# A causal convolution by Toeplitz matmuls moved from 64x128 to 64x64 tiles of TensorE, in front of an RWKV channel mix

## The chip, the core and the metric

The kernel runs on one core of a Trainium2 chip. The metric is the device time of one execution in microseconds (us), over several runs. The profile is one execution taken by the hardware profiler. Its engines are PE (TensorE, matmuls; PEld its weight loads), ACT (ScalarE), DVE (VectorE), POOL (GpSimd) and SP (SyncE, which here only issues DMA).

## The reference

Eight sequences of 4160 tokens with 192 channels. First a causal depthwise convolution with 7 taps: the 192 channels are 8 heads of 24, and all channels of a head share their taps, which come from a softmax over the head's 7 weights.

```python
w = softmax(weight)                       # (8 heads, 7 taps)
x_pad = concat(zeros(6 tokens), x)        # causal
y[b, s, h, g] = sum_k w[h, k] * x_pad[b, s + k, h, g]
```

Then the channel mix of RWKV on y:

```python
y_prev = y shifted by one token
xk = mu_k * y + (1 - mu_k) * y_prev       # mu: one value per channel
xr = mu_r * y + (1 - mu_r) * y_prev
k = max(xk @ w_k, 0)                      # 192 -> 1024
v = (k * k) @ w_v                         # 1024 -> 192
out = sigmoid(xr @ w_r) * v               # w_r: 192 -> 192
```

## The kernel before

The sequences go in four pairs; the two of a pair (index `s`, or `st`) lie on partitions 0 to 63 and 64 to 127 when their channels are contracted 64 at a time. TensorE therefore works in tiles of 64 rows x 128 columns: two of them, one on either half of the partitions, run side by side in the array.

**Steps, slots, bundles.** A pair is cut into steps of 512 tokens (256 at the two ends of the first pair). A step has 8 slots, each computing 128 of the 1024 channels of k for both sequences. Four slots make a bundle, so that a step takes two bundles. There are 65 bundles, then the rest of V. The program writes every engine's instructions in the order of the text below (the schedule is manual).

**PSUM.** All results of matmuls go through one ring of four tiles. A tile is two banks wide, [...]. The fifth tile takes the place of the first, and so on.

```python
ring = ctx.enter_context(tc.tile_pool(name="ring", bufs=4, space=bass.MemoryType.PSUM))
... ring.tile([P, 2, BANK], FP32, tag="k", ...)        # P = 128, BANK = 512
```

**The convolution.** x is loaded in groups of up to 10 blocks. A block has 128 tokens on the partitions, of which 120 are new (`BLK = 120`, 6 are the halo). `toe[:, h, :]` is the banded Toeplitz matrix of head h, 128 x 128. The contraction over the 128 tokens of a block is done in two halves of 64 rows (`i`), both of which add to the same outputs. Two row tiles that run side by side write different banks: in the first half of a unit, row tile i writes bank i, in the second half they change places. Between the halves a nop on ACT (`clobber_nop`) makes the second wait for the first, so that no two row tiles meet in one bank. A group of 10 blocks has four units of two heads; `conv_out` casts the unit's results to bf16 and puts the channels in the order that the mix needs.

```python
groups = []                       # (pair, first block, blocks, first bundle that needs it, on_pe)
for p in range(NPAIR):
    blk0 = 0
    for nb, s, on_pe in (
        ((3, 0, True), (4, 1, True), (4, 2, True), (5, 3, True), (10, 4, False), (9, 6, False))
        if p == 0
        else ((10, 0, False), (10, 2, False), (10, 4, False), (5, 7, False))
    ):
        groups.append((p, blk0, nb, first_bundle[first_step[p] + s], on_pe))
        blk0 += nb

def conv_units(g):                # heads that go into bank 0 and bank 1
    if groups[g][2] * 4 * G <= BANK:                      # up to 5 blocks
        return [((0, 1), (6, 7)), ((2, 3), (4, 5))]
    return [((0,), (1,)), ((3,), (4,)), ((6,), (7,)), ((2,), (5,))]

def conv_mm(g, c, half):
    ...
    for k in range(last + 1):
        for i in range(2):
            q = slice(i * Q, (i + 1) * Q)                 # Q = 64
            bank = (i + half) % 2
            h = unit[bank][k]
            nc.tensor.matmul(                             # line 300
                out=banks[:, bank, :, :, k * G : (k + 1) * G],
                lhsT=toe[q, h, :],
                rhs=xbs[g][q, :nb, :, h * G : (h + 1) * G],     # nb * 2 * 24 columns
                start=half == 0 and k == 0, stop=half == 1 and k == last)
    if half == 0:
        nc.scalar.clobber_nop([nc.scalar.lower_ap(conv_ps[g, c])])
```

The groups marked `on_pe` (the first four of the first pair) get to the mix by TensorE alone. The others ("large groups") go by way of DRAM: y is written there token by token (`y_write`) and read back transposed (`y_read`), channels on the partitions.

**K, R and V.** A k tile is three pairs of 512-column matmuls, followed by a relu on ACT and a square on DVE. R of 256 tokens is six pairs of 192 columns, followed by a sigmoid on ACT. V is 32 pairs of 192 columns in two halves, with the same change of banks and the same nop between them, and is multiplied by R's sigmoid on DVE.

```python
def k_relu(n):
    ...
    nc.scalar.activation(out=k_sb, in_=ps..., func=AF.Relu)          # line 499
def r(s, j):
    ps = ring.tile(...)
    ...                                                             # matmuls: line 544
    r_sbs[s, j] = three.tile([P, 2, 2 * D], BF16, tag="r_sb", name="r_sb")
    nc.scalar.activation(out=r_sbs[s, j], in_=ps[:, :, 0 : 2 * D], func=AF.Sigmoid)
def v_rows(s, j, half, ks=(0, 1)):
    ...                                                             # matmuls: line 572
    if half == 0:
        nc.scalar.clobber_nop([nc.scalar.lower_ap(v_ps[s, j])])
```

**A bundle** (`units` are the units of the convolution that this bundle has; `run(mix_...)` are DVE's steps of the mix; the parts for bundle 2 are cut):

```python
def bundle_rest(b, ns):
    units = xt.get(b, []) + [None, None]
    quad = vq.get(b, [None])[0]
    for n in bundles[b - 1][2:]:
        k_square(n)
    run(mix_a, b)
    k_mm(ns[0]); k_relu(ns[0]); k_square(ns[0])
    run(mix_b, b)
    conv_half(units[0], 0)          # first half of a unit
    k_mm(ns[1])
    conv_half(units[0], 1)          # second half, then its casts on ACT
    k_relu(ns[1]); k_square(ns[1])
    run(rq, b)                      # R; from bundle 7 on, of the next bundle's V
    v_rows(*quad, 0)
    k_mm(ns[2]); k_relu(ns[2])
    conv_half(units[1], 0)
    v_rows(*quad, 1)
    conv_half(units[1], 1)
    run(mix_c, b)
    k_mm(ns[3]); k_relu(ns[3])
    v_out(*quad)                    # the product with R on DVE, and the store
    run(late, b)
```

In the first pair the units of the large groups stand in bundles 2 to 5, two in each. In the other pairs a group's units stand one in each of successive bundles, from ten bundles before the group is needed: `xs = range(fb - 10, fb - 10 + nx)`. In bundles 6 to 53 this makes 42 bundles with one unit and 6 with none; bundles 54 to 64 have none.

Of the kernel before, what the change touches and what calls it, by code (L numbers as in the profile page):

```python
# [14 lines left out]
def kernel(  # L15
# [11 lines left out]
    nc = tc.nc  # L27
# [9 lines left out]
    HALO = K - 1  # L37
    BLK = 120
    GB = 10
    NBLK = -(-S // BLK)  # L40
    BANK = 512
    STEP = 512
    TAIL = S % 128
# [42 lines left out]

    groups = []
    for p in range(NPAIR):
        blk0 = 0
        for nb, s, on_pe in (  # L90
            ((3, 0, True), (4, 1, True), (4, 2, True), (5, 3, True), (10, 4, False), (9, 6, False))
            if p == 0
            else ((10, 0, False), (10, 2, False), (10, 4, False), (5, 7, False))
        ):
            groups.append((p, blk0, nb, first_bundle[first_step[p] + s], on_pe))
            blk0 += nb


    xbs = {}

    def x_tile(g):
        p, blk0, nb, _, _ = groups[g]
        xb = three.tile([P, GB, 2, D], BF16, tag="xb", name="xb")
        xbs[g] = xb
        if g > 4:

            nc.vector.memset(xb[0:1, 0, 0, 0:2], 0.0)
        if blk0 == 0:
            nc.gpsimd.memset(xb[0:32, 0, :, :], 0.0)
        if blk0 + nb == NBLK:  # L110
            nc.gpsimd.memset(xb[:, nb - 1, :, :], 0.0)

    def load_x(g):
        p, blk0, nb, _, _ = groups[g]
        xb = xbs[g]
        for s in range(2):
            b = 2 * p + s
            lo, hi = 0, nb
            if blk0 == 0:
                lo = 1  # L120
                nc.gpsimd.dma_start(out=xb[HALO:P, 0, s, :], in_=x[b, 0 : P - HALO, :])
            t0 = blk0 * BLK - HALO
            if blk0 + nb == NBLK:
                hi = nb - 1
                r0 = t0 + hi * BLK
                nc.gpsimd.dma_start(out=xb[0 : S - r0, hi, s, :], in_=x[b, r0:S, :])
            nc.gpsimd.dma_start(  # L127
                out=xb[:, lo:hi, s, :],
                in_=bass.AP(
                    tensor=x.tensor,  # L130
                    offset=x.offset + (b * S + t0 + lo * BLK) * D,
                    ap=[[D, P], [BLK * D, hi - lo], [1, D]],
                ),
            )

    def load_x_first(eng, q0, q1, n0, n1, s0, s1):

# [138 lines left out]
    ys, yTs, y_drams = {}, {}, {}  # L276
    conv_ps = {}

    def conv_units(g):

        if groups[g][2] * 4 * G <= BANK:
            return [((0, 1), (6, 7)), ((2, 3), (4, 5))]
        return [((0,), (1,)), ((3,), (4,)), ((6,), (7,)), ((2,), (5,))]
# [42 lines left out]
                        )  # L326

    def to_yT(g, c, o, b0, b1, copy):
        c0 = YC + (groups[g][1] + b0) * BLK
        copy(out=yTs[0][:, c, c0 : c0 + (b1 - b0) * BLK], in_=o[:, 0 : (b1 - b0) * BLK])  # L330

    def conv_out(g, c, copy):
# [24 lines left out]
            )  # L357

    def new_yT(p):
        yTs[p] = two.tile([P, 3, -(-(YC + NBLK * BLK) // 16) * 16], BF16, tag="yT", name="yT")  # L360
        y_drams[p] = dram.tile([NBLK * BLK, 2 * D], BF16, tag=f"y{p % 2}", name="y_dram")
        nc.vector.memset(yTs[p][:, :, 0:YC], 0.0)


    def y_write(g):
        p, blk0, nb, _, _ = groups[g]
        if blk0 == 0:
            new_yT(p)
        nc.sync.dma_start(
            out=y_drams[p][blk0 * BLK : (blk0 + nb) * BLK, :].rearrange("(n t) c -> t n c", t=BLK),  # L370
            in_=ys[g][:BLK, :nb, :],
        )

    def y_read(g):
        p, blk0, nb, _, _ = groups[g]
        r0, r1 = blk0 * BLK, min((blk0 + nb) * BLK, S)
        nc.sync.dma_start_transpose(
            out=yTs[p][:, :, YC + r0 : YC + r1], in_=y_drams[p][r0:r1, :]
        )


    def tr(g, j):

        p, blk0, nb, _, _ = groups[g]
        ps = ring.tile([P, 2, 2 * BANK], BF16, tag="k", name="ps_t")
        todo = range(4 * j, min(nb, 4 * j + 4))
        view = ps[:, :, 0 : 6 * BLK].rearrange("p b (c i t) -> p b c i t", c=3, i=2)
        for i0 in todo[::2]:
            for c in range(3):
                for i in range(i0, min(nb, i0 + 2)):  # L390
                    nc.tensor.transpose(
                        out=view[:, (i - 4 * j) // 2, c, i % 2, :],
                        in_=ys[g][:BLK, i, c * P : (c + 1) * P],
                        identity=ident[:BLK, :BLK],
                    )

        for i in todo[::2]:
            n = min(2, nb - i)
            c0 = YC + (blk0 + i) * BLK
            (nc.scalar.copy if g == 3 and j == 0 else nc.vector.tensor_copy)(  # L400
                out=yTs[p][:, :, c0 : c0 + n * BLK].rearrange("p c (n t) -> p c n t", n=n),
                in_=view[:, (i - 4 * j) // 2, :, :n, :],
            )
# [116 lines left out]
            vb = max(vb, last_bundle[s]) + 1  # L520
            quads.append((s, j, vb))

    r_sbs = {}

    def v_mm(o, s, t):
        for f in range(NF):
# [9 lines left out]
    def r(s, j):  # L536
        xr = xrs[s]
        ps = ring.tile([P, 2, BANK], FP32, tag="k", name="ps_r")
        for k in range(2):
            ts = slice((2 * j + k) * P, (2 * j + k + 1) * P)  # L540
            for c in range(NC):
                for i in range(2):
                    q = slice(i * Q, (i + 1) * Q)
                    nc.tensor.matmul(  # L544
                        out=ps[:, i, k * D : (k + 1) * D],
                        lhsT=xr[q, c, ts],
                        rhs=wr[q, c, :],
                        start=c == 0,
                        stop=c == NC - 1,
                    )  # L550
        r_sbs[s, j] = three.tile([P, 2, 2 * D], BF16, tag="r_sb", name="r_sb")
        nc.scalar.activation(out=r_sbs[s, j], in_=ps[:, :, 0 : 2 * D], func=AF.Sigmoid)  # L552

    v_ps = {}

# [65 lines left out]
            )  # L621


    early, rq, xt, mix_a, mix_b, mix_c, vq, late = ({} for _ in range(8))

    def at(table, b, fn, *a):
        table.setdefault(b, []).append((fn, a))
# [4 lines left out]
            if half == 1:  # L632
                conv_out(*unit, nc.scalar.copy)

    for g, (p, blk0, nb, fb, on_pe) in enumerate(groups):
        if g < 3:
            continue
        nx = len(conv_units(g))
        if p == 0:
            xs = {3: [1, 1], 4: [2, 2, 3, 3], 5: [4, 4, 5, 5]}[g]  # L640
        else:
            xs = range(fb - 10, fb - 10 + nx)
        for i, b in enumerate(xs):
            xt.setdefault(b, []).append((g, i))
        if not on_pe:
            at(late, xs[-1], y_write, g)

            at(mix_c if g == 4 else late, xs[-1] + (1 if g < 6 else 2), y_read, g)
        if g > 4:

            b = {5: 1, 6: 2, 7: 7}.get(g)
            b = first_bundle[first_step[p]] + (-15, -11, -7, -3)[(g - 6) % 4] if b is None else b
            table = {5: mix_a, 7: mix_c}.get(g, early)
            at(table, b, x_tile, g)
            at(table, b, load_x, g)
# [28 lines left out]
            at(late, fb - 1, keep_tail, p)  # L684
    for s, j, vb in quads:
        at(rq, vb if vb < 7 else vb - 1, r, s, j)
        if s == LAST:
            at(late, vb, v_last, s, j)
        else:
            vq.setdefault(vb, []).append((s, j))  # L690
# [117 lines left out]

    def bundle_rest(b, ns):

        units = xt.get(b, []) + [None, None]
        quad = vq.get(b, [None])[0]
        for n in bundles[b - 1][2:]:
            k_square(n)
# [3 lines left out]
        k_square(ns[0])  # L818
        if b > 2:
            run(mix_b, b)  # L820
            conv_half(units[0], 0)
        k_mm(ns[1])
        if b > 2:
            conv_half(units[0], 1)
        k_relu(ns[1])
        if b > 2:
            k_square(ns[1])
        run(rq, b)
        if quad:
            v_rows(*quad, 0)  # L830
        if b == 2:
            tr(3, 0)
            tr(3, 1)
            k_square(ns[1])
            run(mix_b, b)
        k_mm(ns[2])
        k_relu(ns[2])
        if b == 2:
            v_rows(*quad, 1, (0,))
            k_mm(ns[3])  # L840
            k_relu(ns[3])
            conv_half(units[0], 0)
            v_rows(*quad, 1, (1,))
            run(mix_c, b)
            v_out(*quad)
            conv_half(units[0], 1)
            conv_half(units[1], 0)
            conv_half(units[1], 1)
        else:
            conv_half(units[1], 0)  # L850
            if quad:
                v_rows(*quad, 1)
                conv_half(units[1], 1)
            run(mix_c, b)
            k_mm(ns[3])
            if not quad:
                conv_half(units[1], 1)
            k_relu(ns[3])
        if quad and b > 2:
            v_out(*quad)  # L860
# [2 lines left out]
    with tc.manual_schedule():  # L863
        prologue()
        for b in range(-20, 0):
            for table in (early, rq, xt, mix_a, mix_b, mix_c, vq, late):
                assert b not in table, b
        for b in range(quads[-1][2] + 1):
            run(early, b)
# [6 lines left out]
            else:  # L876
                if b == len(bundles):
                    for n in bundles[-1][2:]:
                        k_square(n)
                run(rq, b)  # L880
                for q in vq.get(b, ()):
                    v(*q)
                    v_out(*q)
# [31 lines left out]
```

## Time and profile before

| | |
|---|---|
| time, median of 3 | 417.19 us (417.04 to 417.88) |
| span of the profiled execution | 416.1 us |
| granted TensorE clock | 0.998 |
| mean DMA rate | 155 GB/s |

A page of the profile lists the share of the span in which each engine is busy, then groups of instructions: line, engine, operation, output <- inputs, partitions x elements, count | busy us, mean ns of one | idle time of the engine just before them, and what ended most of it. A timeline lists instructions in order of time: start in us from the span's start, length, engine, line, operation, and how many in a row are put together; a bracket at the end gives idle time ahead of it and who ended it. Matmuls are pipelined: the next one starts before the last one has ended, so that the time of a stretch is read from the starts.

### The profile page before, as it was taken

How to read it: one execution, taken by the hardware profiler on the slowest of the kernel's cores; microseconds unless marked ns; L12 is line 12 of the kernel's file. 1: busy time of each engine (PE TensorE's matmuls, PEld its weight loads, DVE VectorE, ACT ScalarE, POOL GpSimd, SP SyncE). 2: the span in 40 equal slices, each digit the busy share in tenths (PEclk: the TensorE clock that was granted, in tenths of full speed). 3: DMA queues.
4: the chain of work that ended last, by engine and by line, in shares of the span. 5: the costliest groups of instructions: out<-in, count | busy, mean ns of one | idle time of the engine just before them, and what ended most of it. 6: DMA issues, size and time to landing. Idle time of an engine off the chain costs nothing.

```text
span 416.1 us, 16339 instructions
## 1 busy us (share of the span) xinstructions
PE 407.4 (98%) x7125; PEld 317.2 (76%) x7126; DVE 377.8 (91%) x671; ACT 348.2 (84%) x409; POOL 50.7 (12%) x77
## 2 busy tenths in 40 slices
PE   7999999999999999999999999999999999999995
PEld 5567777777878777777777877777787778777795
DVE  5979799999999999999999999999999999999973
ACT  6899888889888888988988898898898788877771
POOL 8640003002030100202021010202000000000000
PEclk9999999999999999999999999999999999999999
DMA  9999889968499793959689593898856464421123
GB/s 143 174 191 204 163 221 189 237 146 163 124 185 215 170 196 102 180 155 176 167 166 206 149 218 106 140 212 166 170 101 161 131 147 125 119 79 55 61 80 115
DMA packets 134298, 64.59 MB, mean 155 GB/s; under 512 B 84158, under 2 KB 134226, under 8 KB 134226
## 3 DMA queue, kind: packets, MB, share of 16 engines
q1 hardware_dynamic: 95138, 48.32, 45.3%
q0 software_dynamic: 38288, 14.66, 31.1%
q8 instruction: 56, 0.92, 0.9%
q10 hardware_dynamic: 800, 0.57, 0.5%
q14 instruction: 16, 0.13, 0.1%
HBM read 29.89 MB, written 36.99 MB: 161 GB/s over the span
## 4 chain that ended last, share of the span: by engine, by line
PE 92%; DVE 3%; ACT 2%; DMA 1%; issue 1%; SPq 0%; ACTq 0%
PE ps_v L572 40%; PE ps_k L487 38%; PE ps_r L544 7%; PE ps_c L300 5%; ACT k_sb L499 1%; PE ps_v L527 1%; DMA mu_raw<-in_moe_mu_r_dram 1%; DVE d L425 1%; DVE k L513 1%; ACT y L346 1%; DVE o_sb L588 0%; DVE xr L461 0%; DVE xk L438 0%; DVE yT L330 0%; PE ps_t L320 0%
## 5 line engine op out<-in xcount | busy, mean ns | idle before, releaser
L499 ACT ACTIVATE k_sb<-ps_k 128x1024 bf16<-128x1024 f32 x260 | 261.3, 1040 | 53.3 <-PE ps_k L487 52.5
L487 PE MATMUL ps_k<-xk,wk 64*128 64x512 bf16 (+1 forms) x1632 | 200.7, 368 | 0.5 <-ACT k_sb L499 0.3
L513 DVE TENSOR_TENSOR k<-k_sb 128x1024 bf16<-128x1024 bf16 x260 | 177.9, 688 | 15.0 <-ACT k_sb L499 7.8
L572 PE MATMUL ps_v<-wv,k 64*128 64x192 bf16 x4032 | 189.0, 243 | 0.3 <-ACT y L346 0.2
L572 PEld LDWEIGHTS <-k 64*128 64x128 bf16 x4032 | 172.6, 94 | 13.4 <-issue 0.8
L487 PEld LDWEIGHTS <-wk 64*128 64x128 bf16 x1632 | 88.4, 94 | 50.7 <-issue 0.4
L588 DVE TENSOR_TENSOR o_sb<-ps_v,r_sb 128x768 f32<-128x768 f32 x64 | 61.2, 957 | 11.6 <-PE ps_v L572 5.3
L552 ACT ACTIVATE r_sb<-ps_r 128x768 bf16<-128x768 f32 x65 | 54.8, 846 | 0.0
L127 POOL DMA_DIRECT2D xb<-in_x_dram x34 | 30.6, 903 | 192.7 <-PE ps_c L300 93.1
L346 ACT CAST y<-ps_c 120x960 bf16<-120x960 f32 (+4 forms) x67 | 50.7, 788 | 1.8 <-PE ps_c L300 1.8
L544 PEld LDWEIGHTS <-xr 64*128 64x128 bf16 x780 | 36.0, 94 | 11.1 <-DVE xr L467 0.3
L544 PE MATMUL ps_r<-wr,xr 64*128 64x192 bf16 x780 | 43.9, 243 | 0.0
L300 PE MATMUL ps_c<-xb,toe 64*128 64x480 bf16 (+2 forms) x240 | 39.2, 335 | 0.8 <-DMA xb<-in_x_dram 0.4
L461 DVE TENSOR_SCALAR xr<-d,mu 128x512 bf16<-128x512 bf16 (+1 forms) x102 | 35.6, 354 | 0.0
L425 DVE TENSOR_TENSOR d<-yT 128x1536 bf16<-128x1536 bf16 (+3 forms) x37 | 31.4, 849 | 1.5 <-ACT yT L330 1.3
L461 DVE TENSOR_SCALAR xk<-d,mu 128x512 bf16<-128x512 bf16 (+1 forms) x98 | 32.7, 361 | 0.1
L467 DVE TENSOR_TENSOR xr<-xr,yT 128x1536 bf16<-128x1536 bf16 (+1 forms) x33 | 31.0, 939 | 1.1
L467 DVE TENSOR_TENSOR xk<-xk,yT 128x1536 bf16<-128x1536 bf16 (+2 forms) x34 | 30.4, 897 | 0.1
L300 PEld LDWEIGHTS <-toe 64*128 64x128 bf16 x240 | 13.5, 94 | 13.0 <-issue 1.6
L409 POOL COPY y_tail<-yT 128x195 bf16<-128x195 bf16 x4 | 1.7, 425 | 68.8 <-DMA yT<-y_dram 68.8
L320 PEld LDWEIGHTS <-xb 128*32 128x32 bf16 (+3 forms) x264 | 5.4, 120 | 2.1 <-ACT xb L221 1.1
L320 PE MATMUL ps_t<-toe,xb 128*32 128x120 bf16 (+3 forms) x264 | 6.6, 273 | 0.2 <-DVE toe L270 0.2
(56 smaller groups left out, 57.6 us busy)
## 6 DMA issues: line engine op xcount, KB each, us to landing
out_dram<-o_sb SPq DMA_DIRECT2D x128, 192.0 KB, 2.6
y_dram<-y SPq DMA_DIRECT2D x10, 900.0 KB, 7.0
xb<-in_x_dram POOLq DMA_DIRECT2D x14, 480.0 KB, 7.9
xb<-in_x_dram POOLq DMA_DIRECT2D x6, 432.0 KB, 8.5
xb<-in_x_dram POOLq DMA_DIRECT2D x10, 192.0 KB, 4.9
y_dram<-y SPq DMA_DIRECT2D x3, 450.0 KB
y_dram<-y SPq DMA_DIRECT2D x1, 810.0 KB
xb<-in_x_dram POOLq DMA_DIRECT2D x2, 384.0 KB, 10.4
```

The lines of the kernel that those rows point to most:

```text
L300: nc.tensor.matmul(out=banks[:, bank, :, :, k * G : (k + 1) * G], lhsT=toe[q, h, :], rhs=xbs[g][q, :nb, :, h * G : (h + 1) * G], start=hal ...
L346: copy(out=bass.AP(tensor=y.tensor, offset=y.offset + d0, ap=[y.ap[0], [d1 - d0, 2], [2 * D, nb], [Q, 2], [1, n]],), in_=bass.AP(tensor=ps ...
L425: nc.vector.tensor_tensor(out=shaped(s, diffs[s][:, cs, :L]), in0=y_of(s, cs, 1), in1=y_of(s, cs, 0), op=ALU.subtract)
L461: nc.vector.tensor_scalar(out=t[:, c, :L], in0=diffs[s][:, c, :L], scalar1=mu[:, i, c : c + 1], scalar2=None, op0=ALU.mult)
L467: nc.vector.tensor_tensor(out=o, in0=o, in1=y_of(s, sl, 0), op=ALU.add)
L487: nc.tensor.matmul(out=ps[:, i, f * L : (f + 1) * L], lhsT=wk[r, c, fs], rhs=xk[r, c, :L], start=c == 0 and f == 0, stop=c == NC - 1 and f ...
L499: nc.scalar.activation(out=k_sb, in_=ps.rearrange("p a b -> p (a b)"), func=AF.Relu)
L513: nc.vector.tensor_tensor(out=o, in0=i, in1=i, op=ALU.mult)
L544: nc.tensor.matmul(out=ps[:, i, k * D : (k + 1) * D], lhsT=xr[q, c, ts], rhs=wr[q, c, :], start=c == 0, stop=c == NC - 1,)
L552: nc.scalar.activation(out=r_sbs[s, j], in_=ps[:, :, 0 : 2 * D], func=AF.Sigmoid)
L572: nc.tensor.matmul(out=v_ps[s, j][:, bank, k * D : (k + 1) * D], lhsT=k2s[s][q, f, t * P : (t + 1) * P], rhs=wv[q, f, :], start=half == 0 ...
L588: nc.vector.tensor_tensor(out=o_sb.rearrange("p (b t) d -> p b (t d)", b=2), in0=v_ps.pop((s, j)), in1=r_sbs.pop((s, j)), op=ALU.mult,)
```

## The change

Each large group's convolution goes into tiles of 64 rows x 64 columns, [...]. The tokens are cut into sub-blocks of 56 new tokens with 64 rows each (`HB = 56`), so that a contraction of 64 rows gives a whole result: nothing is added across the halves, and the nop goes. A group of nb blocks now has 2 nb sub-blocks, half of them on the upper 64 partitions. For one head four matmuls cover the group: by the half of the partitions (`i`, which is also the bank) and by the half of the blocks (`j`, which is the half of the output's partitions). Each has nb / 2 * 48 columns. A large group of 10 holds 1120 tokens instead of 1200, and the last groups become larger to make up for it: 10 instead of 9 blocks in the first pair, 8 instead of 5 in the others. All have four units of two heads.

As a change between tilings is not free, two units stand together in one stretch behind k1, and, from the second pair on, only in every second bundle. The second unit's casts and R's sigmoid come behind the nop between the halves of V, so that the nop is not held up by them. Loads of x come in two parts for the two halves of the partitions, and writes of y in four.

```diff
-            ((3, 0, True), (4, 1, True), (4, 2, True), (5, 3, True), (10, 4, False), (9, 6, False))
+            ((3, 0, True), (4, 1, True), (4, 2, True), (5, 3, True), (10, 4, False), (10, 6, False))
             if p == 0
-            else ((10, 0, False), (10, 2, False), (10, 4, False), (5, 7, False))
+            else ((10, 0, False), (10, 2, False), (10, 4, False), (8, 6, False))
 ... (load_x)
+        if on_pe:
+            parts, step, rows = ((0, base),), BLK, P
+        else:
+            parts, step, rows = ((0, base), (Q, base + nb * HB)), HB, Q
 ... (new)
+    def conv_tiles(g, c):
+        nb = groups[g][2]
+        ...
+        ps = ring.tile([P, 2, BANK], FP32, tag="k", name="ps_c")
+        m = nb // 2
+        banks = ps[:, :, 0 : m * 4 * G].rearrange("p i (m s c) -> p i m s c", m=m, s=2)
+        for k in range(2):
+            h = 2 * c + k
+            for i in range(2):
+                q = slice(i * Q, (i + 1) * Q)
+                for j in range(2):
+                    nc.tensor.matmul(
+                        out=banks[j * Q : (j + 1) * Q, i, :, :, k * G : (k + 1) * G],
+                        lhsT=toe[q, h, q],
+                        rhs=xbs[g][q, j * m : (j + 1) * m, :, h * G : (h + 1) * G],
+                        start=True,
+                        stop=True,
+                    )
+    def conv_tiles_out(g, c):
+        ...   # one cast for units 0 and 3, two for units 1 and 2
 ... (y_write)
-        nc.sync.dma_start(
-            out=y_drams[p][blk0 * BLK : (blk0 + nb) * BLK, :].rearrange("(n t) c -> t n c", t=BLK),
-            in_=ys[g][:BLK, :nb, :],
-        )
+        for j in range(2):
+            for i in range(2):
+                r0 = base + (i * nb + j * m) * HB
+                nc.sync.dma_start(
+                    out=y_drams[p][r0 : r0 + m * HB, :].rearrange("(n t) c -> t n c", t=HB),
+                    in_=ys[g][j * Q : j * Q + HB, i * m : (i + 1) * m, :],
+                )
 ... (r: the sigmoid goes into a function of its own)
+    def r_out(s, j):
 ... (schedule)
-            xs = range(fb - 10, fb - 10 + nx)
+            xs = [fb - 9] * 2 + [fb - 7] * 2
 ... (bundle_rest, without the parts for bundle 2)
         k_square(ns[0])
         if b > 2:
             run(mix_b, b)
-            conv_half(units[0], 0)
         k_mm(ns[1])
-        if b > 2:
-            conv_half(units[0], 1)
         k_relu(ns[1])
         if b > 2:
             k_square(ns[1])
+            for u in units:
+                conv_tiles(*u)
+            for u in units[:1]:
+                conv_tiles_out(*u)
         run(rq, b)
         if quad:
             v_rows(*quad, 0)
+        if b > 2:
+            for u in units[1:]:
+                conv_tiles_out(*u)
+        run(rs, b)                  # R's sigmoid
         k_mm(ns[2])
         k_relu(ns[2])
-            conv_half(units[1], 0)
             if quad:
                 v_rows(*quad, 1)
-                conv_half(units[1], 1)
             run(mix_c, b)
             k_mm(ns[3])
             k_relu(ns[3])
```

## The prediction

> **What bounds the kernel now.** I read the page's busy shares first, then the timeline of TensorE (PE) in the middle and near the end, then ScalarE (ACT) in the same windows, and last the starts of single matmuls in the trace.
>
> ```profile
> PE 407.4 (98%) x7125; PEld 317.2 (76%) x7126; DVE 377.8 (91%) x671; ACT 348.2 (84%) x409; POOL 50.7 (12%) x77
> L300 PE MATMUL ps_c<-xb,toe 64*128 64x480 bf16 (+2 forms) x240 | 39.2, 335 | 0.8 <-DMA xb<-in_x_dram 0.4
> L346 ACT CAST y<-ps_c 120x960 bf16<-120x960 f32 (+4 forms) x67 | 50.7, 788 | 1.8 <-PE ps_c L300 1.8
> ```
>
> PE is the bound. Its 39.2 us in the convolution (L300) is not what the convolution costs, because overlapping matmuls are counted by their pipelined ends. Starts tell the cost: between the starts of successive pairs of 64-row tiles lie 215.7 ns for 512 columns (k) and 82 ns for 192 (R and V). [...] so 480 columns are 202.5 ns. From 76 us to 406 us the starts follow this sum without one gap over 30 ns: **PE streams, and only columns cost**. A whole bundle from the middle, PE (start, length, engine, line, operation):
>
> ```profile
> 202.43 1.48 PE L487 MATMUL ps_k<-xk,wk 64*128 64x512 bf16 x12
> 203.73 0.38 PE L300 MATMUL ps_c<-xb,toe 64*128 64x480 bf16 x2
> 203.93 0.83 PE L487 MATMUL ps_k<-xk,wk 64*128 64x512 bf16 x6
> 204.58 0.38 PE L300 MATMUL ps_c<-xb,toe 64*128 64x480 bf16 x2
> 204.78 0.68 PE L544 MATMUL ps_r<-wr,xr 64*128 64x192 bf16 x12
> 205.29 1.50 PE L572 MATMUL ps_v<-wv,k 64*128 64x192 bf16 x32
> ```
>
> The first twelve are k3 of the bundle before and k0, six each (3 x 215.7 = 0.65 us), so this bundle starts at T = 203.08: k0, half a unit, k1, the other half, R at T+1.70, V at T+2.21. The next one starts at 209.22: 6.14 us. ACT meanwhile:
>
> ```profile
> 203.30 1.94 ACT L499 ACTIVATE k_sb<-ps_k 128x1024 bf16<-128x1024 f32 x2 [0.80 <-PE ps_k L487]
> 205.12 0.97 ACT L346 CAST y<-ps_c 120x960 bf16<-120x960 f32 x1
> 205.96 1.06 ACT L499 ACTIVATE k_sb<-ps_k 128x1024 bf16<-128x1024 f32 x1
> ```
>
> Relu 3 of the bundle before starts at T+0.22 (its matmuls have just ended), relu 0 at T+1.14, the cast at T+2.04, relu 1 at T+2.88. ACT instructions in a row start 0.91 us apart (relu), 0.84 (cast of 960), 0.69 (sigmoid). So **ACT is at its busiest just after T**: three k tiles reach it in 1.9 us of PE time and cost it 2.7. V is close behind: relu 0 ends at 205.24, and V starts at 205.29 in the buffer that relu 0 has freed.
>
> Near the end no convolution is left:
>
> ```profile
> 347.68 2.12 PE L487 MATMUL ps_k<-xk,wk 64*128 64x512 bf16 x18
> 349.62 0.68 PE L544 MATMUL ps_r<-wr,xr 64*128 64x192 bf16 x12
> 350.12 1.50 PE L572 MATMUL ps_v<-wv,k 64*128 64x192 bf16 x32
> ...
> 353.40 2.12 PE L487 MATMUL ps_k<-xk,wk 64*128 64x512 bf16 x18
> ```
>
> Here k3, k0 and k1 run on; from one such run to the next it is 5.73 us, with the same relus and VectorE work. So neither ACT nor VectorE holds a bundle without convolution above 5.73.
>
> Two early stretches show what the change will meet. First, a switch of tiling:
>
> ```profile
> 16.99 0.83 PE L487 MATMUL ps_k<-xk,wk 64*128 64x256 bf16 x12 [0.31 <-ACT k_sb L499]
> 17.75 0.60 PE L320 MATMUL ps_t<-toe,xb 128*32 128x120 bf16 x32
> 18.29 0.39 PE L487 MATMUL ps_k<-xk,wk 64*128 64x256 bf16 x4
> ```
>
> The last k pair starts at 17.536, so the next start was due at 17.645 and came at 17.755: 0.110 us to go in. The last set of four starts at 18.135, 18.188 was due, 18.291 came: 0.103 us to go out. Inside, sets of four 120-column matmuls are 52.5 ns apart: four column tiles stream at once, and their short weight loads hide.
>
> Second, bundle 6, where two R tiles follow k1, so that V takes the fifth buffer after the convolution:
>
> ```profile
> 50.99 1.38 PE L544 MATMUL ps_r<-wr,xr 64*128 64x192 bf16 x24
> 52.55 1.17 PE L572 MATMUL ps_v<-wv,k 64*128 64x192 bf16 x24 [0.18 <-ACT y L346]
> ```
>
> ```profile
> 49.68 1.96 ACT L499 ACTIVATE k_sb<-ps_k 128x1024 bf16<-128x1024 f32 x2
> 51.50 0.99 ACT L346 CAST y<-ps_c 120x960 bf16<-120x960 f32 x1
> ```
>
> Tiles here are k0, c, k1, R, R', V. Relu 0 ends at 51.64; R' starts at 51.69. The cast ends at 52.49; V starts at 52.545. **Each tile waits for the reader of the fourth tile before it, and begins 0.05 us after that reader ends.** These waits cost PE 0.21 and 0.36 us.
>
> [...] in the trace the four of the set at 17.755 start within 10 ns. [...]
>
> **The change, part by part.**
>
> Removed from PE: in the large groups 80 pairs of 480 columns (16.2 us), 8 of 432 (1.46) and 24 of 240 (2.46), 20.1 us. Added: each head of a unit is one set of four 64x64 matmuls. Pair 0 has 2 groups x 8 heads = 16 sets of 240 columns; each other pair 3 x 8 = 24 of 240 and 8 of 192. That is 88 x 102.5 ns + 24 x 82.5 ns = 11.0 us. **Columns save 9.1 us.** There are 28 stretches (4 in pair 0, 8 in each other pair); each goes in and out: 28 x 0.213 = 6.0 us. Were nothing else moved, PE would gain **3.1 us**.
>
> Moved: the order in the ring. A bundle with convolution now takes k0, k1, c, c', R, V, k2, k3. The fourth tile before R is k0 of the same bundle, and the fourth before V is k1. Before, they were k3 of the last bundle and k0. From T on, with the measured steps:
> - PE alone: k0 and k1 end at 1.30, +0.11 switch, +0.41 for four sets, +0.10 switch: R would start at 1.92, V at 2.41.
> - ACT: relu 3 at 0.22, relu 0 at 1.14, relu 1 at 2.04 (where the cast stood). With 1.02 to 1.03 us each they end at 1.24, 2.16 and 3.07.
> - R waits for relu 0: 2.21. V waits for relu 1: **T+3.12**, 0.71 us after PE could have begun.
> - Then first half of V 1.32, k2 0.65, second half 1.32, k3 0.65: next bundle at T+7.06.
>
> Nothing else in it waits longer. The first cast follows relu 1 at 2.95 and ends by 4.0, k2 needs its buffer at 4.44. The nop that separates V's halves falls at about 4.65, V's second half is due at 5.09; this is what the sigmoid behind the nop is for, and it costs nothing, since the R of this bundle is used in the next. Second cast 4.65, sigmoid 5.5, relu 2 6.2, relu 3 at 7.28: ACT has caught up. A bundle without convolution keeps 5.73.
>
> In bundles 6 to 53: after, 24 x 7.06 + 24 x 5.73 = 306.8 us. Before, 42 bundles carried a unit and 6 none: 42 x 6.14 + 6 x 5.73 = 292.2, and 0.57 of waits in bundle 6, which go. **That is +14.0 us.** In pair 0 (bundles 2 to 5) the wait between halves in bundle 2 goes and its columns shrink (-0.5), while bundles 3 to 5 take 1.33 us for convolution and wait in place of 0.73 to 0.96 (with 0.3 us of old waits), and in bundle 3 ACT still has bundle 2's casts before relu 0 (about 0.5 more): +1.5, some **+1.0** together. Sum: 417.2 + 14.0 + 1.0 = **432 us**.
>
> Off the path: ACT gets 14 x 6 = 84 casts in the large groups for 64, some 8 us more; loads come in twice as many pieces and read 128 rows for 112 new tokens, where it was 128 for 120; writes of y come in four pieces. All have whole bundles of time: from pair 1 on a load is issued four to six bundles ahead, and y is read two bundles after it is written.
>
> **The rivals.**
> 1. The columns decide and the ring does not bite: 417.2 - 3.1, about 414, or 413.5 with bundle 6's waits gone. For it: PE has been at its columns for 330 us, and the change was arranged in stretches to save switches. Against it: V starts today within 0.05 us of its buffer's release, and bundle 6 shows the very wait. It would need ACT to reach relu 1 by T+1.3, when k1's matmuls have only just been issued.
> 2. The ring bites and ACT does not catch up: 1.75 us of casts in one bundle push relu 2 and relu 3 beyond the next T. My sum leaves ACT free at 7.1 against relu 3 ready at 7.28, so 0.2 us of slack. If 0.3 us is missing in each of 24 bundles: 439.
> 3. Transfers: more and smaller pieces make the early groups late (the load of the first large group was already waited for at 27.4 us). Worth 1 us once; later loads have slack.
> 4. Sets of 64x64 that do not overlap fully (205 ns for a set instead of 102.5): the wait for relu 1 would hide the 0.41 us more per stretch, so the total hardly moves.
>
> **Range and chances.** The wait of 0.71 us is a difference of measured steps; 0.1 us in it is 2.4 us of the total. That gives 429 to 435; rival 2 stretches the top, and a part of rival 1 (ACT ahead of my walk in some bundles) the bottom: 423 to 437. Slower by over 2% means above 425.5: 0.80. Within 2%: 0.18, nearly all rival 1. Faster than 408.8 needs more than the columns can give: 0.02.
>
> **What would show each step.** In the middle, bundles alternate 7.06 and 5.73 us. The sets of 64x64 matmuls start 102.5 ns apart, with 0.11 and 0.10 us around the stretch (the last hidden in R's wait). R's first matmul starts 0.05 us after the end of relu 0, V's after that of relu 1, 3.1 us after k0's; PE shows idle time released by ACT k_sb ahead of R and V in these bundles. ACT's casts of ps_c rise from 67 to 87 (84, and 3 of the one group that keeps the old way). Alternation at 6.35 and 5.73 would show the ring step wrong; a first V start much later than relu 1's end would point to rival 2 or to something that I don't see.

## The result, and the profile after

The changed kernel takes **432.26 us** (median of 4, 432.0 to 432.38) against 417.53 us for the kernel before, measured beside it: a ratio of 1.0351, with a 95% interval of 1.0333 to 1.0369. It is 3.5% slower. The profiled execution spans 430.5 us.

The lines of the page after that answer to those shown of before: busy shares, then the matmuls of R, V and the convolution, and the casts. (L302 and L319 are the new 64x64 convolution and its casts, L601 is R, L632 is V, L556 the relu.) The second line is the chain that ended last, by engine.

```profile
PE 409.9 (95%) x7349; PEld 313.4 (73%) x7350; DVE 373.0 (87%) x671; ACT 355.4 (83%) x429; POOL 65.1 (15%) x102
...
PE 74%; ACT 12%; issue 5%; DMA 4%; POOL 2%; SPq 1%; DVE 1%; ACTq 0%; DVEq 0%; POOLq 0%
...
L632 PE MATMUL ps_v<-wv,k 64*128 64x192 bf16 x4032 | 189.1, 243 | 6.7 <-ACT k_sb L556 6.6
...
L319 ACT CAST y<-ps_c 128x960 bf16<-128x960 f32 (+5 forms) x84 | 54.0, 684 | 21.7 <-PE ps_v L632 21.7
...
L601 PE MATMUL ps_r<-wr,xr 64*128 64x192 bf16 x780 | 43.6, 243 | 6.1 <-ACT k_sb L556 6.1
...
L302 PE MATMUL ps_c<-xb,toe 64*64 64x240 bf16 (+1 forms) x448 | 16.6, 265 | 0.0
```

The convolution itself has become cheap: 16.6 us busy for the large groups, where L300 had 39.2 (some 1.5 of these for the small group that stays). But R and V now have idle time ahead of them, and what ends it is ACT's relu. ACT is 12% of the chain that ended last. Before, it was 2%:

```profile
PE 92%; DVE 3%; ACT 2%; DMA 1%; issue 1%; SPq 0%; ACTq 0%
```

The idle figures, 6.1 and 6.7 us, are too small: a matmul's modelled end covers a part of the wait (243 ns is listed for one of V, and its pairs start 82 ns apart). Starts show all of it, 10.7 and 11.5 us. A bundle without units and one with two, PE:

```profile
203.61 2.12 PE L544 MATMUL ps_k<-xk,wk 64*128 64x512 bf16 x18
205.56 0.68 PE L601 MATMUL ps_r<-wr,xr 64*128 64x192 bf16 x12
...
209.34 2.12 PE L544 MATMUL ps_k<-xk,wk 64*128 64x512 bf16 x18
211.39 0.60 PE L302 MATMUL ps_c<-xb,toe 64*64 64x240 bf16 x16
212.19 0.67 PE L601 MATMUL ps_r<-wr,xr 64*128 64x192 bf16 x12 [0.20 <-ACT k_sb L556]
213.11 1.50 PE L632 MATMUL ps_v<-wv,k 64*128 64x192 bf16 x32 [0.24 <-ACT k_sb L556]
...
216.39 1.91 PE L544 MATMUL ps_k<-xk,wk 64*128 64x512 bf16 x16
```

And ACT in the bundle with two units:

```profile
210.20 2.85 ACT L556 ACTIVATE k_sb<-ps_k 128x1024 bf16<-128x1024 f32 x3 [0.82 <-PE ps_k L544]
212.93 0.98 ACT L319 CAST y<-ps_c 128x960 bf16<-128x960 f32 x1
214.71 1.02 ACT L319 CAST y<-ps_c 128x320 bf16<-128x320 f32 x2 [0.80 <-PE ps_v L632]
```

From 203.61 to 209.34 it is 5.73 us, from 209.34 to 216.39 it is 7.05. T is again the start of k0. With T = 209.99 (k3's three pairs after 209.34), relu 3, 0 and 1 start at 210.20, 211.12 and 212.03. Relu 0 ends at 212.14 and R starts at 212.19; relu 1 ends at 213.06 and V starts at 213.11.

**The balance on PE**, from the starts of its matmuls, in the 27 bundles with a stretch behind k1: before V gaps of 0.425 us in the mean (11.5), before R 0.396 (10.7, of which about 0.1 each is the switch out), into the stretch 0.109 (2.9). That is 25.1 us. The columns save 8.4 of them in the trace: 9.1 by their count, less 0.7 because the first set of each stretch takes 0.025 us longer. Waits of the kernel before in bundles 2 to 6 that went are 1.5. What is left, 15.2 us, stands against 14.7 between the two medians (0.4 us of switches and a wait in bundles 2 and 3 are not counted).

### The profile page after: what moved, and what is told of

Its sections match the earlier page's. It is cut to its first block, busy times and chain, and to the rows that moved or that the text cites. A ratio compares the mean times of both kernels' runs of the same rounds, so it can differ in the third digit from the quotient of the medians.

```text
span 430.5 us, 16802 instructions
## 1 busy us (share of the span) xinstructions
PE 409.9 (95%) x7349; PEld 313.4 (73%) x7350; DVE 373.0 (87%) x671; ACT 355.4 (83%) x429; POOL 65.1 (15%) x102
## 4 chain that ended last, share of the span: by engine, by line
PE 74%; ACT 12%; issue 5%; DMA 4%; POOL 2%; SPq 1%; DVE 1%; ACTq 0%; DVEq 0%; POOLq 0%
PE ps_v L632 38%; PE ps_k L544 29%; ACT k_sb L556 11%; PE ps_r L601 4%; DMA xb<-in_x_dram 2%; DMA y_dram<-y 2%; PE ps_v L584 1%; PE ps_c L302 1%; SPq L426 1%; POOL xb L136 1%; POOL wk L208 1%; ACT r_sb L612 1%; DVE o_sb L648 0%; SPq L656 0%; ACT y L319 0%
## 5 line engine op out<-in xcount | busy, mean ns | idle before, releaser
L556 ACT ACTIVATE k_sb<-ps_k 128x1024 bf16<-128x1024 f32 x260 | 251.0, 1025 | 29.1 <-PE ps_k L544 27.8
L632 PE MATMUL ps_v<-wv,k 64*128 64x192 bf16 x4032 | 189.1, 243 | 6.7 <-ACT k_sb L556 6.6
L544 PE MATMUL ps_k<-xk,wk 64*128 64x512 bf16 (+1 forms) x1632 | 192.4, 367 | 1.0 <-DMA wk<-in_moe_w_k_dram 0.5
L632 PEld LDWEIGHTS <-k 64*128 64x128 bf16 x4032 | 172.5, 94 | 24.1 <-issue 11.4
L648 DVE TENSOR_TENSOR o_sb<-ps_v,r_sb 128x768 f32<-128x768 f32 x64 | 61.1, 955 | 40.1 <-PE ps_v L632 38.4
L136 POOL DMA_DIRECT2D xb<-in_x_dram x62 | 45.4, 740 | 195.9 <-PE ps_k L544 125.6
L319 ACT CAST y<-ps_c 128x960 bf16<-128x960 f32 (+5 forms) x84 | 54.0, 684 | 21.7 <-PE ps_v L632 21.7
L612 ACT ACTIVATE r_sb<-ps_r 128x768 bf16<-128x768 f32 x65 | 53.0, 816 | 12.0 <-PE ps_v L632 12.0
L601 PE MATMUL ps_r<-wr,xr 64*128 64x192 bf16 x780 | 43.6, 243 | 6.1 <-ACT k_sb L556 6.1
L601 PEld LDWEIGHTS <-xr 64*128 64x128 bf16 x780 | 35.5, 94 | 17.5 <-issue 9.3
L302 PEld LDWEIGHTS <-toe 64*64 64x64 bf16 x448 | 9.6, 106 | 11.6 <-issue 9.9
L302 PE MATMUL ps_c<-xb,toe 64*64 64x240 bf16 (+1 forms) x448 | 16.6, 265 | 0.0
L111 POOL MEMSET xb<- 32x384 bf16 x3 | 1.3, 423 | 41.9 <-PE ps_k L544 41.9
```

Of the source, the lines that this page charges most:

```text
L136: nc.gpsimd.dma_start(out=xb[q0 : q0 + rows, lo:hi, s, :], in_=bass.AP(tensor=x.tensor, offset=x.offset + (b * S + t0 + lo * step) * D, ap ...
L319: nc.scalar.copy(out=bass.AP(tensor=y.tensor, offset=y.offset + d, ap=[y.ap[0], [m * 2 * D, 2], [2 * D, m], [Q, 2], [1, b - a]],), in_=bas ...
L544: nc.tensor.matmul(out=ps[:, i, f * L : (f + 1) * L], lhsT=wk[r, c, fs], rhs=xk[r, c, :L], start=c == 0 and f == 0, stop=c == NC - 1 and f ...
L556: nc.scalar.activation(out=k_sb, in_=ps.rearrange("p a b -> p (a b)"), func=AF.Relu)
L601: nc.tensor.matmul(out=ps[:, i, k * D : (k + 1) * D], lhsT=xr[q, c, ts], rhs=wr[q, c, :], start=c == 0, stop=c == NC - 1,)
L612: nc.scalar.activation(out=r_sbs[s, j], in_=r_ps.pop((s, j))[:, :, 0 : 2 * D], func=AF.Sigmoid)
```

## The experiments

All are edits of the changed kernel, and each ratio is to the kernel before, run beside it.

**1. One unit in each bundle** (`e1_one_unit`).

```diff
-            xs = [fb - 9] * 2 + [fb - 7] * 2
+            xs = range(fb - 10, fb - 6)
```

> The changed kernel, but from pair 1 on one unit in each of four successive bundles instead of two in every second one: 52 stretches instead of 28. Ring theory (R and V of a bundle with two units wait for relu 0 and relu 1 of the same bundle): the fourth tile before V is now k0 again, so V starts at T+2.21 without a wait, and a bundle takes 5.73 + 0.21 for the two switches + 0.21 for two sets = 6.15 us; sum 420 us, although 24 stretches more switch the tiling. Switch theory (the loss belongs to the 64x64 stretches themselves: 15 us lost and 9.1 us of columns not gained over 28 stretches, 0.86 us each): 52 x 0.86 - 9.1, so 453 us. Theory of bunched casts (two units' casts at once are what ACT cannot take): also near 420 us, as they stand one by one; it is not told from the ring here.

Measured: 421.45 us, ratio 1.0092 (1.0077 to 1.0107). Nearly twice the switches, and 11 us less. From pair 1 on R starts straight after the stretch:

```profile
204.35 2.11 PE L544 MATMUL ps_k<-xk,wk 64*128 64x512 bf16 x18
206.38 0.40 PE L302 MATMUL ps_c<-xb,toe 64*64 64x240 bf16 x8
206.72 0.67 PE L601 MATMUL ps_r<-wr,xr 64*128 64x192 bf16 x12
207.22 1.48 PE L632 MATMUL ps_v<-wv,k 64*128 64x192 bf16 x32
```

With T = 205.00 V starts at T+2.22, and no bracket stands at R or V. The switches are not what costs; the second unit in the bundle is. Of the 1.4 us above the 420, 0.6 is in the sum itself (417.2 + 1.0 + 48 x 6.15 - 292.8 = 420.6). Another 0.39 is a wait in bundle 6: with its two R tiles V takes k1's buffer even here (relu 1 ends at 53.21, V starts at 53.26). The 47 bundles behind it take 6.13 to 6.19 us where 6.15 was expected, 0.2 to 0.3 together.

**2. R ahead of the stretch** (`e2_r_first`): `run(rq, b)` moves in front of the two `conv_tiles`.

> The changed kernel with R's matmuls ahead of the stretch instead of behind it. Ring theory: the fourth tile before R is k2 of the last bundle, so R's wait (0.29 us on top of the switch) goes; but the fourth before V is still k1, V still starts when relu 1 ends, at T+3.12, and the time stays: 432 us within 0.7. If the waits of R and V were two costs that add up, taking R's away would save 27 x 0.29 = 8 us: 424 us. Switch theory and bunched casts: 432 us.

Measured: 432.25 us, ratio 1.0351 (1.0334 to 1.0369): the same. PE with T = 209.75:

```profile
209.10 2.12 PE L544 MATMUL ps_k<-xk,wk 64*128 64x512 bf16 x18
211.04 0.67 PE L601 MATMUL ps_r<-wr,xr 64*128 64x192 bf16 x12
211.65 0.71 PE L302 MATMUL ps_c<-xb,toe 64*64 64x240 bf16 x16
212.87 1.50 PE L632 MATMUL ps_v<-wv,k 64*128 64x192 bf16 x32 [0.52 <-ACT k_sb L556]
```

R no longer waits, and V takes up all of the wait: T+3.12 again. The two waits are one, and what fixes it is the end of relu 1.

**3. The sigmoid ahead of the nop** (`e3_sigmoid_early`): `run(rs, b)` moves up, straight behind `run(rq, b)`.

> The changed kernel with R's sigmoid straight behind R's matmuls, ahead of the nop: one part of the change undone. Ring theory: ACT is free for 0.8 us before the end of V's first half, the sigmoid (0.69 us) falls into that, the nop is not later than before, and PE's waits are the same two: 432 us within 1. If the order behind the nop is worth something, V's second half waits for the nop in the bundles with units: 0.2 us or more in each of 27, at least 437 us.

Measured: 432.35 us, ratio 1.0353 (1.0338 to 1.0368): no difference. This part of the change neither helps nor harms: ACT has 0.80 us free ahead of the end of V's first half (the bracket at 214.71 above), and the sigmoid fits in.

**4. A PSUM tile of V's own, and the stretch behind V's first half** (`e4_v_tile`).

```diff
-    ring = ... tc.tile_pool(name="ring", bufs=4, space=PSUM)
+    ring = ... tc.tile_pool(name="ring", bufs=3, space=PSUM)
+    vring = ... tc.tile_pool(name="vring", bufs=1, space=PSUM)   # V in v_rows; the warm-up tile at the start
-            for u in units: conv_tiles(*u)             # behind k1
-            for u in units[:1]: conv_tiles_out(*u)
         run(rq, b)
+        run(rs, b)
         v_rows(*quad, 0)
-            for u in units[1:]: conv_tiles_out(*u)
-        run(rs, b)
+            for u in units: conv_tiles(*u)
+            for u in units: conv_tiles_out(*u)
```

> V gets a PSUM tile of its own (a pool of one), everything else shares a ring of three; the stretch of two units goes behind V's first half, both units' casts behind the nop, R's sigmoid ahead of it. Ring theory: the third tile before R is k3 of the last bundle (relu 3 ends at T+1.24, R is due at 1.30), V waits for the product of the last bundle (long done), the first unit for relu 0, the second for relu 1 (3.07, due 3.42), k2 for the sigmoid (3.8, due 3.73), k3 for the first cast: no wait over 0.1 us, a bundle with units takes 6.35 to 6.45 us, and the sum is 414 to 416.5 us, below the kernel before. Switch theory: 28 stretches as in the changed kernel, 432 us. Bunched casts: ACT has the same two units' casts at once, relu 2 and relu 3 come late, 425 us or more.

Measured: 416.79 us, ratio 0.9986 (0.9979 to 0.9993). PE and ACT around the stretch:

```profile
205.08 0.60 PE L303 MATMUL ps_c<-xb,toe 64*64 64x240 bf16 x16
205.69 0.82 PE L545 MATMUL ps_k<-xk,wk 64*128 64x512 bf16 x6
```

```profile
204.81 0.83 ACT L613 ACTIVATE r_sb<-ps_r 128x768 bf16<-128x768 f32 x1
```

The same 28 stretches, columns and casts as in the changed kernel, and 15.5 us less. So neither the 64x64 tiles nor the bunched casts are the loss. A bundle with units takes 6.44 us, within what was expected: k2 waits 0.07 to 0.15 us for the sigmoid, which ends at 205.64 above. The time is 0.3 us above the range, as a ring of three also waits in bundles 2 to 6 (0.41 us ahead of the second R of bundle 6). Three edits were made here at once, V's tile, the place and the sigmoid: run 3 shows the sigmoid's move alone to do nothing, runs 5 and 6 part the other two.

**5. The place alone** (`e5_late_ring4`): as 4, sigmoid included, but with the one ring of four.

> The place of the last run (stretch behind V's first half, sigmoid ahead of the nop) but with the ring of four for all tiles, V's too. Ring theory: R, V and both units find their buffers free, but now k3 is the fourth tile after V, and V is free only when its product is done: 0.2 us after the last matmul of V's second half, 0.96 us of product, 0.05: k3 waits 1.2 us, a bundle with units takes 7.6 us, and the sum is 447 us (443 to 455, if VectorE comes late to the product). If the place alone was the cure and V's own tile has nothing to do with it: 417 us.

Measured: 415.63 us, ratio 0.9957 (0.9943 to 0.997). **My expectation was 31 us off.** PE and VectorE, the product of V being L648:

```profile
205.70 1.50 PE L632 MATMUL ps_v<-wv,k 64*128 64x192 bf16 x32
207.02 2.12 PE L544 MATMUL ps_k<-xk,wk 64*128 64x512 bf16 x18
```

```profile
207.24 0.96 DVE L648 TENSOR_TENSOR o_sb<-ps_v,r_sb 128x768 f32<-128x768 f32 x1 [0.87 <-PE ps_v L632]
```

k3 starts at 207.02, before the product of V has even begun. So k3 is not in V's buffer. The addresses in the compiled programs show why: the four buffers are not used in strict turn. k3 lies in the first unit's buffer, and V's is used by R of the next bundle. In the compiled programs of all eleven kernels here every tile that follows another in a buffer (449 in the kernel before, 455 in each other) lies in that buffer of its pool whose last reader stands first in the program's order, and V's reader (the product) stands last in the bundle. In the changed kernel R still gets k0's buffer and V k1's under this rule, as the addresses and the traces show, so the explanation of its time stands; what falls is "always the fourth tile before".

**6. V's own tile alone** (`e6_v_tile_old_place`): the pools of 4, the order of the changed kernel.

> V's own tile and a ring of three, but the stretch and the order of the changed kernel. Ring theory: the third tile before the second unit is k0 (2.21 us after T), before R it is k1: R starts at T+3.12 instead of 2.21, V's first half at 3.62, its nop at 5.14, so that the second unit's casts end at 6.2 and k2, the third tile after it, starts then instead of at 4.44; k3 follows V's second half at 8.17, the next bundle begins at T+8.81: 1.76 us more than in the changed kernel in 27 bundles, 480 us (470 to 485). If V's own tile alone was the cure: 417 us.

Measured: 447.37 us, ratio 1.0716 (1.0702 to 1.0731).

```profile
207.20 0.40 PE L303 MATMUL ps_c<-xb,toe 64*64 64x240 bf16 x8
208.00 0.40 PE L303 MATMUL ps_c<-xb,toe 64*64 64x240 bf16 x8 [0.40 <-ACT k_sb L557]
208.92 0.67 PE L602 MATMUL ps_r<-wr,xr 64*128 64x192 bf16 x12 [0.52 <-ACT k_sb L557]
209.41 1.50 PE L633 MATMUL ps_v<-wv,k 64*128 64x192 bf16 x32
210.73 0.83 PE L545 MATMUL ps_k<-xk,wk 64*128 64x512 bf16 x6
```

With T = 205.80 the second unit waits for relu 0 (T+2.20) and R for relu 1 (T+3.12), as expected: one buffer fewer moves each wait one tile forward. V follows R without a wait, 0.49 us later than in the changed kernel. But k2 doesn't wait for the second unit's casts. By the rule of run 5 it takes the first unit's buffer, whose cast is done. Taken with that rule, the walk gives 7.05 + 0.49 = 7.54 us a bundle (7.55 in the trace) and 432.3 + 27 x 0.49 = 445.5 us; 447.4 came, with most of the 1.9 us between them ahead of bundle 6 (1.1) and in it (0.4). That part of the expectation failed, in the same way as in run 5. V's own tile is no cure; the place is.

**7 and 8. The stretch behind k2, with V's own tile** (`e7_behind_k2`), **and the second R of bundle 6 there too** (`e8_behind_k2_second_r`). As in run 4, the sigmoid of R stands ahead of V's first half.

```diff
         k_mm(ns[2]); k_relu(ns[2])
+            for u in units: conv_tiles(*u)
+            for u in units: conv_tiles_out(*u)
         v_rows(*quad, 1)
```

> V's own tile and a ring of three, the stretch behind k2, ahead of V's second half. In the run with the stretch behind V's first half k2 still waited 0.07 to 0.09 us for the sigmoid in each of 27 bundles. Here the third tile before k2 is k0, before the units k1 and R, before k3 it is k2 (relu 2 starts at T+4.0, as no cast stands ahead of it). Ring theory: no wait but the two switches, a bundle with units takes 6.35 us, and the sum is 2 us lower than there: 414.9 us (414 to 415.7). If the place does not matter once V has its own tile: 416.8 us.

> As the last one, with the second R of bundle 6 behind k2 instead of behind the first R, where it waited 0.41 us for relu 0 in the trace of the stretch behind V's first half. Ring theory: 0.4 us less than the last one, 414.5 us.

Measured: 416.47 us, ratio 0.9977 (0.9968 to 0.9986), and 416.22 us, ratio 0.9975 (0.9964 to 0.9986). The first misses by 0.8 us. k2's wait is gone, but with a ring of three R of the next bundle takes k3's buffer and starts 0.07 to 0.08 us late 21 times, as relu 3 now runs behind the casts. The expected 0.4 us between the two runs is not resolved by the times; in the traces bundle 6 takes 6.72 and 6.29 us.

**9. The stretch behind k2, one ring of four** (`e9_ring4_behind_k2`): the edit of 7, sigmoid included, without the pools.

> One ring of four, the stretch behind k2, ahead of V's second half. Ring theory, with the rule as the run with the late stretch in a ring of four corrected it (a tile takes the buffer whose reader stands first in the program's order, so the open V is passed over): k2 takes k0's buffer, the units those of k1 and R, k3 that of k2, and R of the next bundle that of V, done long before; nobody waits. The late stretch lost 0.07 to 0.09 us at k2 behind the sigmoid in each of 27 bundles, which goes here: about 2 us less than its 415.6, so 413.6 us (412.8 to 414.6), with only the two switches, 0.11 and 0.10 us, around each stretch. If the waits are not additive or the casts behind relu 2 delay relu 3: 415.5 us or more.

Measured: **413.48 us** (413.20 to 413.71), ratio 0.9902 (0.9883 to 0.9922): 1% faster than the kernel before, 4.3% faster than the changed kernel, by the ratio of the two. PE and ACT:

```profile
202.84 0.81 PE L544 MATMUL ps_k<-xk,wk 64*128 64x512 bf16 x6
203.58 0.60 PE L302 MATMUL ps_c<-xb,toe 64*64 64x240 bf16 x16
204.12 1.49 PE L632 MATMUL ps_v<-wv,k 64*128 64x192 bf16 x32
205.45 2.11 PE L544 MATMUL ps_k<-xk,wk 64*128 64x512 bf16 x18
207.39 0.66 PE L601 MATMUL ps_r<-wr,xr 64*128 64x192 bf16 x12
```

```profile
199.94 2.85 ACT L556 ACTIVATE k_sb<-ps_k 128x1024 bf16<-128x1024 f32 x3 [0.94 <-PE ps_k L544]
202.67 0.83 ACT L612 ACTIVATE r_sb<-ps_r 128x768 bf16<-128x768 f32 x1
203.69 1.02 ACT L556 ACTIVATE k_sb<-ps_k 128x1024 bf16<-128x1024 f32 x1 [0.20 <-PE ps_k L544]
204.62 1.88 ACT L319 CAST y<-ps_c 128x960 bf16<-128x960 f32 x3
```

PE has no gap left there but the two switches (0.093 and 0.103 us around the stretch at 203.58), and no other in any bundle from 34 us to the end of the k tiles. The stretch comes when ACT has caught up with the three relus, so its casts fill ACT's free time, and no matmul waits behind them. This is the gain that the columns promise: 3.1 us by the sum of the prediction, and 0.6 of bundle 6's waits, against 4.0 measured.

## Why the prediction was right

- **The total**: 432.0 predicted, 432.26 measured, and the parts fit too. From bundle 6 to 54 the k0 tiles lie 307.2 us apart, and 293.3 in the kernel before: 13.9 more, 14.0 predicted. (24 x 7.06 + 24 x 5.73 is 307.0, not the 306.8 of the sum; bundle 6's second R of 0.5 is left out both of it and of the sum for before.) In pair 0 bundle 2 takes 0.44 us less and bundles 3 to 5 take 1.63 more (0.5 and 1.5 predicted), so that bundle 6 starts 1.1 us later than before (1.0 predicted).
- **Columns and switches**: right. Sets of four 64x64 matmuls of 240 columns start 0.102 us apart, the four of a set within 10 ns; only the first of a stretch takes 0.127. (The predicted 102.5 ns was an estimate, on the line through the spacings of pairs before: 82.5 ns at 192 columns, 215.7 at 512. Pairs of 480 columns start 202 ns ahead of what follows them there, 202.4 by that line.) Going in costs 0.109. Going out shows alone where nobody waits: 0.102 to 0.103 in bundle 2 of the changed kernel and in run 9.
- **The waits**: right to 0.01 us. R at T+2.20 (2.21 predicted), V at T+3.12 (3.12), bundle 7.05 (7.06), and 5.73 without units. Stretches of 192-column sets are 0.08 us shorter, and their bundles take 7.05 us all the same: time that PE spends before R and V is hidden by the waits, as rival 4 supposed. Runs 1, 2 and 4 to 6 tie the waits to the buffers; run 1 rules out the switches as the loss, run 4 the switches and the bunched casts.
- **The nop and the sigmoid**: that they cost nothing was right (run 3). That this order is needed for V's second half was not shown: without it nothing changes.
- **ACT catches up, loads and writes have time**: right. ACT's casts are 87, its busy time rose by 7.2 us in all (8 predicted for the casts), and relu 3 waits for its matmuls, not for casts: it starts at T+7.27 (7.28 predicted). The chain has 4% of DMA, a part of it on writes of y in the middle, but the bundles there take 7.05 and 5.73 us like the others, and from 60 us to the end of the k tiles PE has no gap over 0.03 us but those at the stretches, R and V.
- **The rule of the ring** was too simple, though its two uses in the prediction held: "each tile waits for the reader of the fourth tile before it" is true where readers stand in the order of their tiles, which bundle 6 of the kernel before could not tell from the true rule. The two expectations that rested on the difference, of runs 5 and 6, were wrong by 31 and 33 us. "The fifth tile takes the place of the first", in the description of the kernel before, is wrong in the same way: there k1 already takes V's buffer, five tiles back, and the unit between k0 and k1 takes that of k2, three back.

Rival 1's 414 us was the size of the gain that the columns hold; it needed another place, not another tiling.

## What to carry to other kernels

Before moving matmuls into one stretch, list for each later tile the buffer that it takes and when that buffer's reader ends; here the added columns cost their length (0.43 us for four sets), but two more tiles ahead of a busy reader cost the reader's backlog (0.72 us more in each of 27 bundles: the gaps of 0.396 and 0.425 less the switch of 0.10). Put a stretch that takes buffers where the engine that frees them has caught up (run 9, 413.48 us), not where it has just been handed three tiles in a row (the changed kernel, 432.26 us). Look the buffers up in the compiled program: in run 5 they were not used in turn, and the expectation that they were was 31 us off.

## What the runs showed of the hardware

- A matmul that waits for a buffer which ACT reads starts 0.05 us after the recorded end of that reader (0.050 to 0.053 in the waits of R, V, k2 and the units, in all kernels here).
- In 64x64 tiles sets of four matmuls start 0.102 us apart at 240 columns and 0.082 at 192, as pairs do in 64x128 tiles (0.103 and 0.082 in the kernel before), with 64-column weight loads of 0.106 us in the mean hidden behind them: the loads of a set start 0.10 us ahead of its matmuls (211.417 and 211.517 in the changed kernel). Only the first set after a switch takes 0.025 us longer; its loads start with it (211.388 and 211.390).
- A change of tiling costs 0.09 to 0.11 us each way, and nothing more where PE waits for a buffer behind it: in the changed kernel R, with a switch ahead of it, starts 0.05 us after its relu, and so does V, with none.
